# A squared-ReLU attention and Fourier-mix FFN kernel on one core: the first FFN layer of two token groups in two passes, with the hand-offs around it reordered

## The chip, the cores and the metric

The kernel runs on 1 core of one Trainium2 chip. The metric is the time of one execution in device microseconds (us); lower is better. The kernel before takes 610.42 us, the median of 3 runs (609.92 to 610.85).

## The reference

Eight batches of 448 tokens. Twelve heads of 64 attend with squared ReLU, the result is mixed by a two-dimensional Fourier transform of which the real part is kept, and a normalised FFN of width 3072 is added.

```python
scores = (1/sqrt(64)) * q @ k.T                  # per batch (8) and head (12), 448 x 448
x  = (maximum(scores, 0)**2 / 448) @ v           # heads side by side: x is 8 x 448 x 768
u  = x + real(fft(fft(x, axis=1), axis=2))
un = (u - mean(u)) / sqrt(var(u) + 1e-6)         # over the 768 features of a token
out = u + maximum(un @ w_ch1, 0) @ w_ch2         # 768 -> 3072 -> 768
```

## The kernel before

Data are bf16 for TensorE (PE) and f32 for `u` and the output. The names follow the data:

- `turn_on_pe` (batches 0 and 1) and `turning` (later ones) lay q and k out with the head dimension on partitions (`qkT`). On PE a set is 16 small matmuls into one `psF` bank, which VectorE (DVE) or ScalarE (ACT) copies out.
- `attention(b)` visits 24 score blocks of a batch, three at a time. A block is two matmuls at L537 into `psS`; ACT takes the ReLU (L558) and DVE squares it (L564) into one of nine `sq` buffers. A value set, eight matmuls at L522, uses four squares of an earlier visit; `lag` says how many visits old they must be. `fold` brings the result to SBUF (`xT`, L445 and L448).
- `mix(b)` multiplies by the channel table (L961), casts to `pc`, and `mix_rows(b, ch)` makes the rows of one half in two parts `ch`: matmuls at L805, `tm` and `tp` on DVE, `u` on DVE and GpSimd (POOL), statistics, `std`, `nmr`, and the normalised rows `un`. From batch 2 on `un` is stored to DRAM (`ntop`, `nbot`) and comes back turned by DMA as `unT`; for batch 1 PE turns it (`turn_rows`, L775).
- `first_tail` does all of this for batch 0 in an order written out by hand: four row tiles `t` (`rows`, L605 and L609), their statistics (L629), copies of `u` (L658), `un` (L682 on POOL, L684, L687), a turn on PE (L708) and an unload into `unT` (L723). At L706 and L713 it issues 24 matmuls on a constant tile, `warm`, between the turns.
- `ffn(b)` takes a group of 384 or 512 tokens, which alternate. FFN1 (L1073) is 24 output blocks `j` of six matmuls, each block a `psF` bank, then a ReLU to `hT` (L1044, L1046). FFN2 (L1091) is 48 matmuls for each 128 tokens, in two halves of 384 columns, each added to a reloaded `u` (`o`, L1054) and stored.

PSUM is held in three double banks (`BS`, tiles `psS`) and two single banks (`BF`, tiles `psF`). FFN1, FFN2, the value sets and the turned q and k all take turns on the two `psF` banks.

The order on each engine is fixed when the kernel is built. Every piece of work is a generator that asks for an engine, a duration, what it waits for and the buffers that it takes; `Streams.run` gives the engine to the piece that can begin first by its own cost functions, and keeps that order:

```python
def mm(n):
    return n / 2400 + 0.006
...
key = (ok is not None and not ok(), max(t), s[1][eng != "PE"])
```

`ok` in `attention` holds a visit back until the FFN has progressed far enough (`lead`); for batch 1 also until the tail of batch 0 is through (`tail`). On the chip each engine then works through its list in order, and a wait at its head holds all that is behind it. The DMA queues of SyncE (SP) and POOL are such lists too: a DMA on POOL waits until the one eight places before it has landed, and a second indirect store into the same DRAM tile waits for the first.

Of the kernel before, what the change touches and what calls it, by code (L numbers as in the profile page):

```python
# [12 lines left out]
ALU = mybir.AluOpType  # L13
# [104 lines left out]
def mm(n):  # L118
    return n / 2400 + 0.006
# [18 lines left out]
def kernel(  # L138
# [54 lines left out]
    back = [const.tile([128, 1], mybir.dt.int32, name=f"back{i}") for i in range(2)]  # L193
    warm = const.tile([128, 512], BF16, name="warm")
# [27 lines left out]
    def mirrors():  # L222
        nc.gpsimd.memset(rev, 0.0)
        nc.gpsimd.affine_select(out=rev, in_=rev, compare_op=ALU.not_equal, fill=1.0,
                                base=-127, pattern=[[1, 128]], channel_multiplier=1)
        nc.gpsimd.iota(back[0], pattern=[[0, 1]], base=HS, channel_multiplier=-1)

        v = const.tile([128, 2], FP32, name="backv")
# [253 lines left out]
    def attention(b):  # L482
# [5 lines left out]
        while pa < NB:  # L488
# [4 lines left out]
            lag = 3 if few else 1  # L493
# [18 lines left out]
            e = yield need("PE", dur + SWITCH, deps, bufs, lambda: progress[0] >= lead and (b != 1 or tail[0] == 2 or tail[0] == 0 and p < 0))  # L512
# [68 lines left out]
    def first_tail(pcs):  # L581


        pus, helds, done, sts = [None] * 4, [None] * 4, [[None, None] for _ in range(4)], [None] * 4
        mvs, stds, rss, nms, uts, pts = ([None] * 4 for _ in range(6))
        t_st, t_mv, t_std, t_rn = ([0.0] * 4 for _ in range(4))
        t_un, t_u = [[0.0, 0.0] for _ in range(4)], [[0.0, 0.0] for _ in range(4)]

        def rows(t):
            ch, i = divmod(t, 2)  # L590
            s0, s1 = SC[ch]
            n = s1 - s0
            d = 4 * mm(D // 2) + 3 * 0.06
            e = yield need("PE", 2 * d, [pcs[0][1], pcs[1][1]] + x_ready[0], [BF, BF] if t == 3 else [BS])
            if t == 3:
                pu = helds[t] = [BF.take() for _ in range(2)]
            else:
                helds[t] = [BS.take()]
                pu = [helds[t][0][:, 0], helds[t][0][:, 1]]
            for hf in range(2):  # L600

                for w in range(2):
                    for a, (n0, n1) in enumerate(TC):
                        mat = seq[:n1 - n0, w, a, s0:s1] if w == 0 or i ^ hf else nseq[:n1 - n0, a, s0:s1]
                        nc.tensor.matmul(pu[hf][:n, 0:D // 2], lhsT=mat,  # L605
                                         rhs=pcs[a][0][:n1 - n0, w, hf:hf + D // 2],
                                         start=(w == 0 and a == 0), stop=False)
                for a in range(3):
                    nc.tensor.matmul(pu[hf][:n, a * 128:(a + 1) * 128],  # L609
                                     lhsT=xTc[5 - a if hf else a][:, i * XH + s0:i * XH + s1],  # L610
                                     rhs=rev if hf else ident, start=False, stop=(a == 2))
                done[t][hf] = e - (1 - hf) * d + LATENCY["PE"]
            pus[t] = [p[:n] for p in pu]
            if t == 3:
# [5 lines left out]
        def half(t, hf):  # L620

            return pus[t][hf][:, D // 2 - 1::-1] if hf else pus[t][hf][:, 0:D // 2]

        def stats(t, hf):
            n = SC[t // 2][1] - SC[t // 2][0]
            t_st[t] = yield need("DVE", dve(D // 2), [done[t][hf]])
            if hf == 0:
                sts[t] = work.tile([128, 2, 6], FP32, name="stats", tag="stats", bufs=2)
            nc.vector.bn_stats(sts[t][:n, hf, :], pus[t][hf][:, 0:D // 2])  # L629

        def aggregate(t):
            n = SC[t // 2][1] - SC[t // 2][0]
            t_mv[t] = yield need("DVE", 0.2)
            mvs[t] = work.tile([128, 2, 2], FP32, name="mv", tag="mv", bufs=4)[:n]
            nc.vector.bn_aggr(mvs[t][:, 0, :], sts[t][:n])

        def root(t):
            n = SC[t // 2][1] - SC[t // 2][0]
            t_std[t] = yield need("ACT", 0.25, [t_mv[t] + LATENCY["DVE"]])
            stds[t] = work.tile([128, 2], FP32, name="std", tag="std", bufs=4)[:n]  # L640
            nc.scalar.activation(stds[t][:, 0:1], mvs[t][:, 0, 1:2], AF.Sqrt, bias=eps_t[:n])

        def scale(t):
            n = SC[t // 2][1] - SC[t // 2][0]
            e = yield need("DVE", 0.3, [t_std[t] + LATENCY["ACT"]])
            t_rn[t] = e + LATENCY["DVE"]
            rss[t] = work.tile([128, 2], FP32, name="rstd", tag="rstd", bufs=4)[:n, 0:1]
            nms[t] = work.tile([128, 2], FP32, name="nmr", tag="nmr", bufs=4)[:n, 0:1]
# [3 lines left out]
        def copy(t, hf, en):  # L652
            ch, i = divmod(t, 2)
            n = SC[ch][1] - SC[ch][0]
            e = yield need(en, (act if en == "ACT" else dve)(D // 2), [done[t][hf]], [BU[i]] if hf == 0 else [])
            if hf == 0:
                uts[t] = work.tile([128, D], FP32, name="u", tag=f"u{i}" if i else "u", bufs=2)
            (nc.scalar.copy if en == "ACT" else nc.vector.tensor_copy)(  # L658
                uts[t][:n, hf * (D // 2):(hf + 1) * (D // 2)], half(t, hf))
            t_u[t][hf] = e  # L660
            if t == 3:
                BF.give(helds[t][hf], e)
            if hf == 1:
                if t != 3:
                    BS.give(helds[t][0], max(t_u[t]))
                e = max(t_u[t])
                first_us[ch][i] = uts[t], e + LATENCY["ACT"], e
                u_done[ch][i].t = e + LATENCY["ACT"]

        def norm(t, hf, en):  # L670
            ch, i = divmod(t, 2)
            n = SC[ch][1] - SC[ch][0]
            deps = [t_rn[t]]
            if en == "POOL":
                deps.append(u_done[ch][i])
            d = {"ACT": act(D // 2), "DVE": dve(D // 2), "POOL": 2.0}[en]
            e = yield need(en, d, deps, [BUN[ch]] if i == 0 and hf == 0 else [])
            if uns[0][t] is None:
                uns[0][t] = work.tile([128, D], BF16, name="un", tag=f"un{t}", bufs=1)
            un = uns[0][t][:n]  # L680
            if en == "POOL":
                nc.gpsimd.tensor_scalar(un, uts[t][:n], rss[t], nms[t], op0=ALU.mult, op1=ALU.add)  # L682
            elif en == "ACT":
                nc.scalar.activation(un[:, hf * (D // 2):(hf + 1) * (D // 2)], half(t, hf), AF.Identity,  # L684
                                     bias=nms[t], scale=rss[t])
            else:
                nc.vector.tensor_scalar(un[:, hf * (D // 2):(hf + 1) * (D // 2)], half(t, hf), rss[t], nms[t],  # L687
                                        op0=ALU.mult, op1=ALU.add)
            t_un[t][hf] = e + LATENCY[en]
            if min(t_un[t]) or en == "POOL":  # L690
                half_un[ch][i].t = max(t_un[t])

        def turned_cols(t):

            return ((128, ident, 0, 128), (128, rev[:, 0:63], HS + 97, 63),
                    (96, ident[:96, :96], 128, 96), (97, rev[:97, 31:128], HS, 97))[t]

        def turn(t, k):
            n, idn, c0, w = turned_cols(t)
            un = uns[0][t]  # L700
            e = yield need("PE", 6 * 0.06 + 0.11 * k, [max(t_un[t])], [BS])
            pts[t] = [BS.take()]
            bank = [pts[t][0][:, 0], pts[t][0][:, 1]]
            for i in range(k):

                nc.tensor.matmul(bank[0][:, 0:256], lhsT=warm[:, 0:128], rhs=warm[:, 0:256], start=True, stop=True)  # L706
            for m in range(MC):
                nc.tensor.matmul(bank[m // 3][:, m % 3 * 128:m % 3 * 128 + w], lhsT=un[:n, m * 128:(m + 1) * 128],  # L708
                                 rhs=idn, start=True, stop=True)
            done[t] = [e + LATENCY["PE"]] * 2  # L710
            for i in range(16 if t == 1 else 0):

                nc.tensor.matmul(bank[0][:, 384:512], lhsT=warm[:, 0:128], rhs=warm[:, 0:128], start=True, stop=True)  # L713
            if t == 1:
                yield need("PE", 16 * 0.055)

        def unload(t, en):
            n, idn, c0, w = turned_cols(t)
            g = groups[0][2]
            src = pts[t][0][:, :, 0:384].rearrange("p h (m w) -> p h m w", w=128)[:, :, :, 0:w]  # L720
            dst = g[:, :, c0:c0 + w].rearrange("p (h m) w -> p h m w", h=2)
            last = yield need(en, (act if en == "ACT" else dve)(6 * w), [done[t][0]])
# [440 lines left out]
```

## Time and profile before

| what | value |
|---|---|
| median of 3 runs | 610.42 us (609.92 to 610.85) |
| span of the profiled execution, first to last instruction | 607.4 us |
| PE busy | 595.4 us, 98% of the span |
| DVE, ACT, POOL busy | 339.4, 293.3, 155.2 us |
| FFN1, FFN2 on PE (L1073, L1091) | 227.2, 225.0 us |
| scores, value sets on PE (L537, L522) | 52.3, 45.9 us |
| first FFN1 matmul of group 0, of group 1, of group 2 | 53.74, 126.67, 210.84 us |
| PE idle after the first FFN1 matmul, up to 604.0 us | 4.73 us |

The profile gives the execution by its span alone; the runs' median stands 3.0 us above it, and that is taken as what lies around the span. A profile line has the start (us), the duration (us), the engine, the source line, the operation, what it writes and reads, how many, and in brackets how long the engine had been idle before it and what ended that wait. A matmul's duration includes the time in which the next ones already run; the distance from one start to the next is what it costs PE.

### The profile page before, as it was taken

The page shows a single profiled execution, that of the slowest core. Times are in us where ns is not written, and L with a number is a line of the kernel's source. Part 1 is how long each engine was busy: PE and PEld are TensorE (multiplying, and loading weights), DVE is VectorE, ACT ScalarE, POOL GpSimd, SP SyncE. Part 2 cuts the span into 40 slices and gives each one's busy share as a digit, 9 for nine tenths or more (in the row PEclk, how much of TensorE's full clock was granted, in tenths as well). Part 3 has the DMA queues.
Part 4 walks back from the last instruction along what each step waited for, and adds up shares of the span by engine and source line. Part 5 has one row for each costly group of instructions (what it writes and reads, how often), then busy time and mean ns, then how long its engine had stood idle before and what let it go on. Part 6 is the DMA issues. An engine that isn't in the chain of part 4 may idle for free.

```text
span 607.4 us, 10224 instructions
## 1 busy us (share of the span) xinstructions
PE 595.4 (98%) x4035; PEld 329.5 (54%) x4054; DVE 339.4 (56%) x766; ACT 293.3 (48%) x445; POOL 155.2 (26%) x200
## 2 busy tenths in 40 slices
PE   8999999989999999999999999999999999999997
PEld 7566556534555565555445565555445566654464
DVE  6977785876596568455834369645843447110011
ACT  5967661677544357436653167435761345014300
POOL 8433203311163137111710117210620006100000
PEclk9999999999999999999999999999999999999999
DMA  9999997888659967977593796985451215420022
GB/s 127 207 209 228 216 194 132 186 128 120 111 148 212 157 121 215 141 135 120 172 154 96 127 127 173 160 164 97 145 136 60 87 51 165 121 91 20 1 79 79
DMA packets 125216, 82.22 MB, mean 135 GB/s; under 512 B 76272, under 2 KB 113168, under 8 KB 125168
## 3 DMA queue, kind: packets, MB, share of 16 engines
q0 software_dynamic: 40320, 34.07, 34.4%
q1 hardware_dynamic: 84848, 47.50, 33.6%
q8 instruction: 32, 0.52, 0.4%
q14 instruction: 16, 0.13, 0.1%
HBM read 62.91 MB, written 26.69 MB: 148 GB/s over the span
## 4 chain that ended last, share of the span: by engine, by line
PE 83%; DVE 11%; ACT 4%; issue 1%; DVEq 0%; ACTq 0%
PE psF L1091 33%; PE psF L1073 32%; PE psF L522 6%; PE psS L537 6%; DVE sq L564 2%; PE psS L961 2%; ACT sq L558 2%; DVE stats L837 2%; PE psS L1113 1%; PE psS L805 1%; DVE u L826 1%; DVE u L825 1%; PE psS L605 1%; PE psF L421 1%; DVE tm L816 1%
## 5 line engine op out<-in xcount | busy, mean ns | idle before, releaser
L1073 PE MATMUL psF<-unT,w 128*128 128x384 bf16 (+1 forms) x1134 | 227.2, 352 | 1.4 <-issue 0.2
L558 ACT ACTIVATE sq<-psS 112x896 bf16<-112x896 f32 x192 | 164.8, 916 | 130.5 <-PE psS L537 130.4
L1091 PE MATMUL psF<-w,hT 128*128 128x384 bf16 (+2 forms) x1343 | 225.0, 326 | 0.8 <-DVE xT L448 0.7
L1091 PEld LDWEIGHTS <-hT 128*128 128x128 bf16 x1344 | 129.2, 98 | 93.4 <-issue 8.8
L1073 PEld LDWEIGHTS <-w 128*128 128x128 bf16 x1152 | 109.6, 98 | 109.3 <-issue 12.3
L1046 ACT ACTIVATE hT<-psF 128x512 bf16<-128x512 f32 (+1 forms) x180 | 98.6, 548 | 110.2 <-PE psF L1073 109.6
L564 DVE TENSOR_TENSOR sq<-sq 112x896 bf16<-112x896 bf16 x192 | 117.8, 635 | 44.6 <-ACT sq L558 43.3
L1054 DVE TENSOR_TENSOR o<-psF,o 128x384 f32<-128x384 f32 (+2 forms) x56 | 31.0, 553 | 106.2 <-PE psF L1091 105.9
L300 POOL DMA_DIRECT2D vn<-in_v_dram x24 | 17.3, 719 | 177.4 <-PE psF L522 156.9
L445 DVE TENSOR_SCALAR xT<-psF 128x224 bf16<-128x224 f32 x48 | 18.7, 389 | 71.7 <-PE psF L522 71.7
L537 PE MATMUL psS<-qkT 64*112 64x448 bf16 x384 | 52.3, 366 | 2.0 <-DVE unT L780 0.8
L522 PE MATMUL psF<-sq,vn 112*64 112x448 bf16 x384 | 45.9, 359 | 1.7 <-DVE sq L564 1.2
L825 POOL TENSOR_TENSOR u<-tp,xn 128x385 f32<-128x385 f32 (+1 forms) x14 | 15.5, 1108 | 117.0 <-DVE tp L816 94.7
L537 PEld LDWEIGHTS <-qkT 64*112 64x112 bf16 x384 | 20.8, 125 | 27.6 <-issue 21.6
L522 PEld LDWEIGHTS <-vn 112*64 112x64 bf16 x384 | 17.9, 109 | 24.2 <-issue 16.0
L854 POOL TENSOR_SCALAR un<-u,rstd,nmr 128x768 bf16<-128x768 f32 (+1 forms) x24 | 26.9, 1124 | 6.4 <-DVE nmr L846 6.0
L837 DVE BATCH_NORM_STATS2 stats<-u 128x6 f32<-128x384 f32 (+1 forms) x56 | 28.2, 539 | 0.0
L879 POOL DMA_INDIRECT ubot<-u,back x16 | 17.1, 1072 | 23.7 <-DVE hT L1044 19.3
L300 POOL DMA_DIRECT2D qn<-in_q_dram x21 | 15.3, 726 | 19.7 <-DVE qkr L389 10.8
L1113 PE MATMUL psS<-warm 128*128 128x126 bf16 (+1 forms) x204 | 17.9, 242 | 1.3 <-DVE warm L215 1.3
L448 DVE TENSOR_SCALAR xT<-psF 128x224 bf16<-128x224 f32 x48 | 18.4, 384 | 0.0
L456 DVE TENSOR_TENSOR fold<-xT 128x225 bf16<-128x225 bf16 x48 | 15.9, 331 | 2.1
(117 smaller groups left out, 369.1 us busy)
## 6 DMA issues: line engine op xcount, KB each, us to landing
out_dram<-o SPq DMA_DIRECT2D x27, 384.0 KB, 2.7
vn<-in_v_dram POOLq DMA_DIRECT2D x24, 224.0 KB, 5.0
qn<-in_q_dram POOLq DMA_DIRECT2D x21, 224.0 KB, 6.3
kn<-in_k_dram POOLq DMA_DIRECT2D x21, 224.0 KB, 7.2
w<-in_moe_w_ch_dram POOLq DMA_DIRECT2D x12, 384.0 KB, 14.1
w<-in_moe_w_ch_dram POOLq DMA_DIRECT2D x4, 1152.0 KB, 22.7
utop<-u SPq DMA_DIRECT2D x8, 384.0 KB, 2.6
o<-utop SPq DMA_DIRECT2D x8, 384.0 KB, 4.5
```

The costliest lines, as they stand in the source:

```text
L300: nc.gpsimd.dma_start(out=t, in_=src[b, hs].rearrange("h (p j) d -> p h (j d)", j=4))
L522: nc.tensor.matmul(av[h * Dh:(h + 1) * Dh, 0:S], lhsT=vn[:, c, h0 + h, :], rhs=sq[:, h, :], start=(c == 0), stop=(c == 3))
L537: nc.tensor.matmul(sc[:R, h, 0:S].rearrange("k (c q) -> k c q", c=4), lhsT=kT[ps, m % 2, c, :], rhs=qT[ps, m % 2], start=True, stop=True)
L558: nc.scalar.activation(r, sc[:R, :, 0:S], AF.Relu)
L564: nc.vector.tensor_tensor(r, r, r, op=ALU.mult)
L837: nc.vector.bn_stats(stats[:n, hf, :], u[:n, hf * (D // 2):(hf + 1) * (D // 2)])
L854: nc.gpsimd.tensor_scalar(un[:n], u[:n], rstd[:n, i:i + 1], nmr[:n, i:i + 1], op0=ALU.mult, op1=ALU.add)
L1046: nc.scalar.activation(h[:, 0:N], ph[:, 0:N], AF.Relu)
L1054: nc.vector.tensor_tensor(o[:, hs], pc[:, 0:w], o[:, hs], op=ALU.add)
L1073: nc.tensor.matmul(ph[:, 0:N], lhsT=w1_sb[m][hf][:, jj * 128:(jj + 1) * 128], rhs=unT[:, m, 0:N], start=(m == 0), stop=(m == MC - 1))
L1091: nc.tensor.matmul(pc[:, 0:w], lhsT=hT[j][:, c * 128:(c + 1) * 128], rhs=w2_sb[j // 6][:, j % 6, hs], start=(j == 0), stop=(j == JC - 1))
L1113: nc.tensor.matmul(first_pps[0][:, t, c0:512], lhsT=warm[:, 0:128], rhs=warm[:, c0:512], start=not begun, stop=False)
```

## The change

**Cost function.** `mm` adds 0.002 instead of 0.006, which moves the planned order in all batches.

**Batch 0's tail.** Each half row is a step of its own. Tile 0 lies in the two `psF` banks, tile 1 in two double banks, one a half; tiles 2 and 3 lie each in one double bank with both halves. Tile widths become 128, 128, 96, 96 (before: 128, 128, 112, 112). `un` of tiles 0 and 1 is made half on ACT, half on DVE, no longer on POOL. The turn goes into the bank that the row came from. Tiles 2 and 3 are streams of their own behind the first FFN1 matmuls: two copies on ACT, then two statistics, and POOL makes `un`. The constant matmuls of L706 and L713 are gone. The row stores wait for the copies; both indirect stores also wait for tile 3's `un`.

**FFN1.** Group 0 is done in a pass over 128 tokens (four blocks `j` in a bank), which needs tile 0 alone, and a pass over 256 (two blocks). Group 1 is done in two passes of 256, the first of which needs three of its five parts. `hT` becomes six tiles of four blocks. The tokens of both groups are in another order, so reloads and stores of `o` are cut into `pieces`.

**Attention.** `lag` is 2 for batches 1 and 2; batch 1 no longer has early work before the tail; batch 2 waits until batch 1's last rows are placed.

```diff
-    return n / 2400 + 0.006
+    return n / 2400 + 0.002
...
-            lag = 3 if few else 1
+            lag = 3 if few else 2 if b < 3 else 1
...
-            e = yield need("PE", dur + SWITCH, deps, bufs, lambda: progress[0] >= lead and (b != 1 or tail[0] == 2 or tail[0] == 0 and p < 0))
+            e = yield need("PE", dur + SWITCH, deps, bufs, lambda: progress[0] >= lead and (b != 1 or tail[0] == 2) and (b != 2 or un_ready[1][1].t is not None))
...
+        widths = (128, 128, R - 16, R - 16)
...
+        def rows(t, hf):
+            i, n = t % 2, widths[t]
+            pool = BF if t == 0 else BS
...
+            pu = held[t][-1][:n] if t == 0 else held[t][-1][:n, hf if t > 1 else 0]
...
+        def store(t):
+            ch, i = divmod(t, 2)
+            n = widths[t]
+            if i:
+                e = yield need("POOL", 1.1, [copied[t], used[3]])
+                nc.gpsimd.indirect_dma_start(
...
-        for t in range(3):
-            yield from rows(t)
-            if t == 2:
-                yield from rows(3)
-            yield from stats(t, 0)
-            if t:
-                yield from scale(t - 1)
-                yield from norm(t - 1, 0, "POOL")
-            yield from stats(t, 1)
-            yield from aggregate(t)
-            yield from copy(t, 0, "ACT")
-            yield from root(t)
-            yield from copy(t, 1, "ACT")
...
-        yield from turn(1, 5)
-        yield from norm(3, 0, "ACT")
-        yield from unload(1, "DVE")
-        yield from turn(2, 3)
...
+        def later(t):
+            for hf in range(2):
+                yield from stats(t, hf)
+            yield from aggregate(t)
+            yield from root(t)
+            yield from scale(t)
+            yield from norm(t, None)
+            for hf in range(2):
+                yield from turn(t, hf)
+            for hf in range(2):
+                e = yield from unload(t, hf)
...
+        yield from run(((rows, 0, 0), (stats, 0, 0), (rows, 0, 1), (copy, 0, 0), (stats, 0, 1), (aggregate, 0),
+                        (copy, 0, 1), (root, 0), (rows, 1, 0), (stats, 1, 0), (scale, 0), (norm, 0, 0), (norm, 0, 1),
+                        (rows, 1, 1), (stats, 1, 1), (aggregate, 1), (rows, 2, 0), (turn, 0, 0), (turn, 0, 1),
+                        (copy, 1, 0), (root, 1), (copy, 1, 1), (scale, 1), (unload, 0, 0), (unload, 0, 1), (rows, 2, 1),
+                        (norm, 1, 0), (norm, 1, 1), (turn, 1, 0), (turn, 1, 1), (unload, 1, 0), (unload, 1, 1)))
         tail[0] = 2
-        sch.add(turn_rows(uns[0][1], max(t_un[1]), 128, rev[:, 63:127], 0, 64, "DVE", second_un[0]), (1, 1))
+        for t in (2, 3):
+            if t == 3:
+                for hf in range(2):
+                    yield from rows(t, hf)
+            sch.add(copies(t), (0.05 * t, 0.05 * t))
+            sch.add(later(t), (0.05 * t, 0.05 * t))
...
+            yield need("SP", 0.0, second_un[:3])
+            group_ready[1].t = max(c.t for c in second_un[:3])
...
-            for t0, n in ((0, 384), (384, 512)):
+            for segs, n in (([(0, 128), (HS + 96, 128), (128, 128)], 384), ([(256, 64), (S, 128), (S + 384, 64), (S + 320, 64), (S + 128, 192)], 512)):
...
-        for j in range(JC):
-            hf, jj = divmod(j, JC // 2)
-            e = yield need("PE", 6 * mm(N), [w1_ready[hf]], [BF])
-            ph = BF.take()
-            for m in range(MC):
-                nc.tensor.matmul(ph[:, 0:N], lhsT=w1_sb[m][hf][:, jj * 128:(jj + 1) * 128],
-                                 rhs=unT[:, m, 0:N], start=(m == 0), stop=(m == MC - 1))
...
+        def first(k, c0, w, ready=()):
+
+            for j0 in range(0, JC, k):
+                hf = j0 // (JC // 2)
+                for i in range(k):
...
+                    for m in range(MC):
+                        nc.tensor.matmul(ph[:, i * w:(i + 1) * w], lhsT=w1_sb[m][hf][:, jj * 128:(jj + 1) * 128],
+                                         rhs=unT[:, m, c0:c0 + w], start=(m == 0), stop=(m == MC - 1))
...
+        if b == 0:
+            yield from first(4, 0, 128, first_un[:1])
+            e = yield from first(2, 128, 256, first_un)
+        elif b == 1:
+            yield from first(2, 0, 256)
+            e = yield from first(2, 256, 256, second_un)
+        else:
+            e = yield from first(1, 0, N)
```

More of the change, by code (lines that the diff above doesn't have):

```diff
@@ L670, in norm @@
[L670 to L706, printed above, removed]
-            for m in range(MC):
[L708 to L722, printed above, removed]
-            (nc.scalar.copy if en == "ACT" else nc.vector.tensor_copy)(dst, src)
-            BS.give(pts[t][0], last)
-            first_un[t].t = last + LATENCY["ACT"]
+            cp(uts[t][:widths[t], hf * (D // 2):(hf + 1) * (D // 2)], half(t, hf))
@@ new lines, in turn, with unload @@
+        def turn(t, hf):
+            n = widths[t]
+            e = yield need("PE", 3 * 0.06, [t_un[t][hf]])
+            for m in range(3 * hf, 3 * hf + 3):
+                nc.tensor.matmul(banks[t][hf][:, m % 3 * 128:m % 3 * 128 + n], lhsT=uns[t][:, m * 128:(m + 1) * 128],
+                                 rhs=rev[:n, 128 - n:] if t % 2 else ident[:n, :n], start=True, stop=True)
+            t_turn[t][hf] = e + LATENCY["PE"]
+        def unload(t, hf):
+            n = widths[t]
+            en, cp = (("ACT", nc.scalar.copy), ("DVE", nc.vector.tensor_copy))[hf]
+            e = yield need(en, (act, dve)[hf](3 * n), [t_turn[t][hf]])
+            src = banks[t][hf][:, 0:384].rearrange("p (m w) -> p m w", w=128)
+            for g, c0, w0, w1 in ((0, t * 128, 0, n),) if t < 3 else ((0, 352, 0, 32), (1, 0, 32, 96)):
+                cp(groups[g][2][:, 3 * hf:3 * hf + 3, c0:c0 + w1 - w0], src[:, :, w0:w1])
+            if t < 2:
+                (BF, BS)[t].give(held[t][hf], e)
+            unloaded[t].append(e + LATENCY[en])
+            if len(unloaded[t]) == 2:
+                first_un[t].t = max(unloaded[t])
+                if t > 1:
+                    BS.give(held[t][0], max(unloaded[t]))
+            return e
@@ L727, in first_tail, with run @@
+        def run(steps):
+            for step, t, *hf in steps:
+                yield from step(t, *hf)
         tail[0] = 1
```

266 lines of the change are left out of this document (141 added, 125 removed).

## The prediction

> **What bounds the kernel now.** I read the page first, then the stretches, then PE's waits and timeline, last the other engines around the places where PE waits.
>
> ```profile
> PE 595.4 (98%) x4035; PEld 329.5 (54%) x4054; DVE 339.4 (56%) x766; ACT 293.3 (48%) x445; POOL 155.2 (26%) x200
> PEclk9999999999999999999999999999999999999999
> ```
>
> PE is the bound, so an edit pays only by taking work off PE or by filling a place where PE waits or runs constants.
>
> ```profile
> 48.00:53.70 5.70, 4.44 (x77) 3.67 (x75) 4.59 (x14) 4.65 (x10) 3.49 (x4) 1.00 1.13 260
> 53.70:90.00 36.30, 35.79 (x284) 19.14 (x279) 27.71 (x62) 25.86 (x37) 5.27 (x7) 1.00 1.22 213
> 90.00:126.70 36.70, 34.52 (x249) 20.55 (x249) 28.30 (x63) 15.49 (x21) 10.33 (x12) 1.00 0.75 153
> 126.70:200.00 73.30, 72.38 (x439) 35.62 (x442) 48.31 (x109) 43.01 (x63) 21.42 (x25) 1.00 0.83 146
> ```
>
> Length less PE's busy time: 1.26 us idle in batch 0's tail, 0.51 in group 0, 2.18 ahead of group 1, 0.92 up to 200 us; from 200 to 604 only 1.12 more. The constants of L706 and L713 in the tail take 0.55, 0.89 and 0.33 us. All that this change could win is therefore 3.0 us in the tail and some 3.6 us behind it.
>
> **The two places.** PE's timeline (start, duration, what; in brackets the idle time before it):
>
> ```profile
> 49.05 1.06 PE L713 MATMUL psS<-warm 128*128 128x128 bf16 x16
> 51.60 0.44 PE L708 MATMUL psS<-rev,un 97*128 97x97 bf16 x6 [0.91 <-ACT un L684]
> 57.45 4.07 PE L1073 MATMUL psF<-unT,w 128*128 128x384 bf16 x24
> 122.58 0.40 PE L537 MATMUL psS<-qkT 64*112 64x448 bf16 x2 [0.83 <-DVE unT L780]
> 124.89 0.38 PE L522 MATMUL psF<-sq,vn 112*64 112x448 bf16 x2 [1.04 <-DVE sq L564]
> 179.70 3.10 PE L1091 MATMUL psF<-w,hT 128*128 128x384 bf16 x18 [0.70 <-DVE xT L448]
> ```
>
> At 122 to 125 us FFN2 of group 0 is used up, group 1 is not complete, and what is left of attention waits for DVE.
>
> **PE's work: about the same.** Starts of successive groups give the price of a matmul. 128 columns: 16 at L713 in 0.89 us, 55.6 ns. 256 columns: 5 at L706 in 0.55 us and 24 at the end of L1091 in 2.6 us, 108.7 ns. 384: 96 at L1073 in 15.7 us, 162.5 ns less its changes. 512: 144 in 31.0 us, 215.3 ns. A change of the kind of work adds 0.10 us (6 of 384 take 1.08).
> I compare what is left in before at its first FFN1 matmul, 53.74 us, with what is left in the changed order of instructions at the turn of tile 2. There group 0's FFN1 has 120 of 128 and 144 of 256 columns left: 6.67 + 15.65 = 22.32 us against 144 x 162.5 ns = 23.40, that is -1.08. Group 1: 288 x 108.7 = 31.30 against 31.00, +0.30. Two turns of 96 rows +0.54, one score block more +0.19, one q-and-k set less -0.52, four more changes of work +0.40. Sum -0.17; I take -0.1. Before leaves 604.1 - 53.74 - 4.73 = 545.6 us of work there, so after leaves 545.5.
>
> **The tail: 0.8 us lost.** Up to 41.06 us nothing differs. The eight half rows go at 0.83 us each. Tile 0, which now has banks of its own, has statistics to 43.79, `nmr` at 44.96, `un` in halves on ACT and DVE (0.68 each, L684 and L687) to 45.68, its turn at 45.73, its unload at 47.10 on ACT and 47.58 on DVE. FFN1 begins at 47.15, six microseconds earlier, with PE waits of 0.22, 0.26 and 0.31. After three blocks come tile 3's rows (48.90 to 50.55), a q-and-k set, a score block and FFN1's fourth block, to 51.73. The next q-and-k set needs a `psF` bank; one is held by FFN1's first four blocks, the other by the first set, until DVE copies it out (L426, 0.61). On DVE that copy stands behind all statistics of tiles 2 and 3, and these are slow for this reason:
>
> ```profile
> 43.23 1.03 DVE L629 BATCH_NORM_STATS2 stats<-psS 128x6 f32<-128x384 f32 x2 [1.41 <-PE psS L609]
> 44.37 0.48 ACT L658 COPY u<-psS 128x384 f32<-128x384 f32 x1 [1.30 <-DVE stats L629]
> 54.22 0.61 DVE L426 COPY qkT<-psF 128x896 bf16<-128x896 bf16 x1
> ```
>
> The first half of that double bank was written by 42.36, yet both readers waited for the whole tile and for one another. Tile 3 sits in such a bank: from 50.75, copy 0.48, statistics 0.57, copy 0.48, statistics 0.57, with 0.05 at each hand-off, to 53.0; then `rstd`, `nmr` and an aggregate for 0.33 and the copy, 53.95. PE waits 2.25 us with everything queued behind it; the set takes 0.52, and the turn of tile 2 comes at 54.55 (POOL's `un`, 0.98 from 53.38, is just in time). That is 0.81 us later than 53.74. If the halves went separately, tile 3 would be 0.5 us earlier: 54.05, the other end.
> The Trainium skill, page "PSUM — Partial Sum Buffer", section "PSUM bank collisions raise a hardware error", asks for a guard between two engines only on the same bank (and quarter of the partitions). By it the halves, which are two banks, need not wait for each other, and the sum would be 0.5 us less. The trace's 43.23 speaks against that here.
>
> **Group 0, 54.5 to 88 us: nothing.** A bank of FFN1 now fills in 1.33 us (24 x 55.6 or 12 x 108.7) and its ReLU of 512 columns takes 0.60 on ACT (L1046) and, from 0.56 for 384, some 0.69 on DVE; they alternate. Copies of `u`, statistics and unloads of tiles 2 and 3 lie under it. I find no wait; the old 0.51 is the other end.
>
> **The step to group 1: 2.2 us won, 0.4 paid.** Adding up pieces puts MIX at 99.0, `mix_rows` at 103.15 and the end of FFN2 at 118.27. In before the last row statistics of batch 1 ended 16.3 us after `mix_rows` began (99.61 to 115.95); without the 1.60 us of squares and a copy between them it is 117.6. ACT's two unloads for the first three parts then end at 118.65: a wait of 0.4 (0 to 1.5). The late `un` (ACT, to 120.8) is needed only by the second pass. Held scores and older squares leave PE with FFN1 to do where it waited for DVE.
>
> **Downstream.** 126.7 to 200: the 0.70 at L1091 came from a value set amid batch 2's rows; that set now comes 13 us instead of 11 after them. I keep 0.3 of 0.92. Group 2 starts at 205.6 instead of 210.84, and its rows begin 10 us later than before, so its DMA chain gets tight:
>
> ```profile
> 190.03 1.21 SPq L477 DMA_TRANSPOSE xn<-xT  x1
> 193.40 1.26 SPq L902 DMA_TRANSPOSE unT<-ntop  x1
> 196.79 1.23 SPq L902 DMA_TRANSPOSE unT<-nbot  x1
> unT<-nbot SPq DMA_TRANSPOSE x9, 4.3
> ```
>
> On SP these two stand right behind the third `xn` transpose of batch 3, at 199.4 to 199.9: 1.2 each, the second issued at 201.8 to 202.4, landing 4.3 later, 206.1 to 206.7. PE waits 0.5 to 1.1 (0 to 1.4 with the drift of both); I take 0.7. From then on the order repeats the old cycle: 1.1.
>
> **Hidden edits.** The last `w1` load lands at 44.4 (29.77 + 14.6), before FFN1. The fourth `w2` load moves ahead of POOL's `un` and both indirect stores behind it: the second lands near 84.5 (78.9 before). SP's reload of `o` waits for it with the third `xn` transpose behind it, which is ready at 82 and wanted by 105; past that, each us of it would delay batch 1's `u`. Two more iotas (0.13 each) lie at 15 us. More, smaller DMAs for `o` go through a queue that is free; `hT` in six tiles frees at the same matmuls.
>
> **The sum.** Start 54.55 + work 545.5 + waits (0 + 0.4 + 0.3 + 0.7 + 1.1 = 2.5) + what follows the last matmul, 3.3 = 605.9 us of span; before, by the same terms, 53.74 + 545.6 + 4.73 + 3.3 = 607.4. That is 1.5 us less, and with the 3.0 between span and median, 608.9 us, -0.25%. About 0.2%, 1.2 us, is what a measurement here can tell from no change: faster is below 609.2, slower above 611.6. With its small terms the forecast goes from 607.9 to 609.9: chance 0.50, 0.36 of it faster.
>
> **Rivals.**
> *More won* (0.12): tile 3's halves go separately and group 2 lands in time: -0.5 - 0.7, 607.7, with 0.5 more from group 1's start and the stretch to 200 down to 606.8.
> *The wait only moves* (0.16; 0.10 the same, 0.06 slower): group 1's last unload or group 2's transposes come 1.5 us later than I walked and the time is 610.4; against it, no sum above has so much missing; for it, ACT and DVE are within 0.5 us of PE at both.
> *The clock, slower* (0.12): the constants that kept PE busy in the tail are gone, and PE now waits 2.25 us at once. The page's clock row never falls, but matmuls of 126 columns at L1113 take 310 ns until 6.4 us and 218 ns at 12 us, with starts 107 and 59 ns apart: after idleness PE is half as fast for 5.4 us. Should the wait bring that back, it costs 2.7 us and the time is 611.6, where it begins to count as slower. Against it: after the waits of 0.91 and 1.04 us nothing is slow.
> The Trainium skill, page "TensorE: Matmul & The Clock Gate", Part 1, has the clock halved after a window of about 3.4 us without work. By that a wait of 2.25 us would not do it; no run here shows where the limit lies.
> *Weights bind narrow matmuls* (0.04): a load lasts 98 ns (PEld at L1073); if each of 144 matmuls of 128 columns took that, +6.1 us, 615. Against it: L708 issued six of 63 columns, each with a load, in 0.17 us.
> *Group 2's chain breaks* (0.06): `nbot` stands behind a v load on POOL; a landing 3.4 us later than walked gives 611.6 or more.
>
> **How the numbers follow.** Faster 0.36 + 0.12 = 0.48, same 0.14 + 0.10 = 0.24, slower 0.06 + 0.12 + 0.04 + 0.06 = 0.28. The range goes from the better rival's end, 606.8, to the clock's case with 0.7 more, 612.3.
>
> **What would show it.** Right: first FFN1 matmul near 47.2; PE idle over 2 us ahead of a q-and-k set at 54, ended by DVE's copy; group 1's FFN1 at 118 to 119; group 2's at 206 with a wait of under 1.1. Wrong: 128-column starts further apart than 56 ns, PE waits over 1 us at 118, or `unT` landing past 208.

## The result, and the profile after

The changed kernel takes 617.25 us, the median of 6 runs (614.05 to 621.14); the kernel before takes 610.22 us in the same measurement (609.10 to 610.87, 6 runs). The ratio is 1.0123 (95% interval 1.0102 to 1.0145): slower by 1.2%, where 608.9 us (606.8 to 612.3) was forecast. Before's runs lie within 1.8 us of each other, after's spread over 7.1 us. The profiled execution of after has a span of 614.0 us and a time of 615.79 us.

The page of after, lines of parts 1, 2 and 5 (in the last: group of instructions, count, busy time, mean ns, idle time before it and what ended most of it):

```profile
PE 595.6 (97%) x4314; PEld 348.9 (57%) x4314; DVE 337.8 (55%) x766; ACT 295.2 (48%) x448; POOL 154.3 (25%) x201
PEclk9999999999999899999999999999999999999999
L1085 PE MATMUL psF<-unT,w 128*128 128x256 bf16 (+3 forms) x1440 | 231.4, 317 | 8.8 <-DMA unT<-nbot 7.3
```

PE has as much to do as before (595.4), as forecast. The clock row, all nines before, has an 8 in the fourteenth slice, and FFN1 now waits 7.3 us for a DMA, at one place.

The same stretches as before the change, and the two behind them (length, then busy time and count of PE, PEld, DVE, ACT and POOL, the granted clock, DMA share, GB/s):

```profile
48.00:53.70 5.70, 3.90 (x56) 3.15 (x54) 3.85 (x12) 3.60 (x9) 0.38 (x1) 1.00 1.15 256
53.70:90.00 36.30, 36.21 (x414) 27.11 (x413) 25.54 (x56) 25.02 (x37) 8.04 (x10) 1.00 1.09 194
90.00:126.70 36.70, 36.36 (x279) 24.00 (x278) 25.22 (x56) 14.76 (x24) 9.72 (x11) 1.00 0.95 163
126.70:200.00 73.30, 73.30 (x572) 47.71 (x572) 49.41 (x112) 41.45 (x59) 21.51 (x24) 1.00 0.80 134
200.00:216.00 16.00, 8.73 (x50) 4.33 (x49) 8.63 (x21) 6.98 (x9) 2.09 (x3) 0.79 1.26 171
216.00:300.00 84.00, 84.00 (x544) 45.61 (x543) 55.72 (x127) 46.85 (x74) 26.89 (x29) 1.00 0.81 150
```

Before, the last two stretches were:

```profile
200.00:216.00 16.00, 16.00 (x107) 8.82 (x104) 10.09 (x27) 6.60 (x10) 3.01 (x5) 1.00 0.90 159
216.00:300.00 84.00, 83.65 (x530) 45.32 (x531) 56.14 (x123) 46.95 (x76) 30.24 (x32) 1.00 0.74 149
```

From 53.7 to 200 us the change does what it was walked to do: between 90 and 126.7 us PE idles 0.34 us where it idled 2.18, and between 126.7 and 200 not at all, where it idled 0.92. In the tail PE idles 0.54 us more than before (1.80 against 1.26). Nearly all of the loss lies from 200 to 216 us: 7.27 us idle, where before had none, and a granted clock of 0.79.

PE's timeline at the three places where the prediction expected waits (start, duration, what; in brackets the idle time before):

```profile
53.79 0.39 PE L424 MATMUL psF<-ident,qn 112*64 112x112 bf16 x8 [1.89 <-DVE qkT L429]
117.90 0.50 PE L1085 MATMUL psF<-unT,w 128*128 128x256 bf16 x3 [0.34 <-DVE unT L780]
212.90 3.68 PE L1085 MATMUL psF<-unT,w 128*128 128x384 bf16 x12 [7.27 <-DMA unT<-nbot]
```

The first two came as forecast (2.25 and 0.4). The third is group 2's FFN1, forecast with 0.7. It also starts at half speed: its first 12 matmuls take 3.68 us.

What stands behind the third, on SP, DVE and POOL, in order of time:

```profile
197.04 0.93 SPq L866 DMA_DIRECT2D ntop<-un  x1
200.79 0.43 DVE L392 COPY qkr<-kn 112x1024 bf16<-112x1024 bf16 x1 [2.21 <-DMA qkT<-qkr]
201.13 0.38 DVE L448 TENSOR_SCALAR xT<-psF 128x224 bf16<-128x224 f32 x1
201.84 1.22 SPq L480 DMA_TRANSPOSE xn<-xT  x1
203.55 1.33 SPq L892 DMA_TRANSPOSE unT<-ntop  x1
204.97 1.26 SPq L892 DMA_TRANSPOSE unT<-nbot  x1
205.23 0.71 POOL L303 DMA_DIRECT2D vn<-in_v_dram  x1 [7.71 <-PE psF L525]
```

The value set whose result goes to `xT` ended on PE near 198.5. DVE reached it only at 201.13, because a copy of k stood ahead of it and waited 2.21 us until an earlier `qkT` transpose had let go of `qkr`. So the third `xn` transpose, walked at 199.4 to 199.9, is issued at 201.84, and both `unT` transposes stand behind it on SP. The first of them also needs the `ntop` store, and by the profile that landed only at 203.46, 6.4 us after its issue at 197.04 and 0.09 us before the transpose went. So without the copy of k the first transpose would still not have gone before 203.5. In e4 below the store landed at 202.08, and the transpose went at 203.22, right behind `xn`: each of the two links alone explains nearly all of the late issue. No run took the copy of k out of the way.
The second transpose is issued at 204.97, and PE goes on at 212.90, 7.9 us later, where 4.3 was walked. 0.26 us after its issue POOL begins to issue 672 KB of q, k and v for batch 4, released by the value set just ahead of FFN1.

### The profile page after: what moved, and what is told of

The parts are those of the page before. It is cut to its first block, busy times and chain, and to the rows that moved or that the text cites. A ratio compares the mean times of both kernels' runs of the same rounds, so it can differ in the third digit from the quotient of the medians.

```text
span 614.0 us, 10759 instructions
## 1 busy us (share of the span) xinstructions
PE 595.6 (97%) x4314; PEld 348.9 (57%) x4314; DVE 337.8 (55%) x766; ACT 295.2 (48%) x448; POOL 154.3 (25%) x201
## 4 chain that ended last, share of the span: by engine, by line
PE 79%; DMA 8%; DVE 6%; POOL 3%; issue 3%; ACT 1%; SPq 0%; POOLq 0%; DVEq 0%; ACTq 0%
PE psF L1085 34%; PE psF L1113 29%; PE psS L540 5%; PE psF L525 5%; DMA w<-in_moe_w_ch_dram 2%; PE psS L954 2%; DMA qn<-in_q_dram 2%; DVE stats L826 2%; DMA unT<-nbot 1%; DMA kn<-in_k_dram 1%; PE psS L794 1%; DMA vn<-in_v_dram 1%; DVE u L815 1%; POOL qk L303 1%; DMA out_dram<-o 1%
## 5 line engine op out<-in xcount | busy, mean ns | idle before, releaser
L1085 PE MATMUL psF<-unT,w 128*128 128x256 bf16 (+3 forms) x1440 | 231.4, 317 | 8.8 <-DMA unT<-nbot 7.3
L1085 PEld LDWEIGHTS <-w 128*128 128x128 bf16 x1440 | 132.4, 98 | 101.1 <-issue 23.3
L303 POOL DMA_DIRECT2D kn<-in_k_dram x21 | 15.2, 725 | 6.8 <-DVE qkr L392 3.2
L1135 PEld LDWEIGHTS <-warm 128*128 128x128 bf16 x206 | 12.8, 104 | 6.3 <-issue 4.6
```

The costliest lines, as they stand in the source:

```text
L303: nc.gpsimd.dma_start(out=t, in_=src[b, hs].rearrange("h (p j) d -> p h (j d)", j=4))
L1085: nc.tensor.matmul(ph[:, i * w:(i + 1) * w], lhsT=w1_sb[m][hf][:, jj * 128:(jj + 1) * 128], rhs=unT[:, m, c0:c0 + w], start=(m == 0), stop ...
L1135: nc.tensor.matmul(first_pps[0][:, t, c0:512], lhsT=warm[:, 0:128], rhs=warm[:, c0:512], start=not begun, stop=False)
```

## The experiments

All kernels below are the changed kernel with the edit shown, except the last, which is the kernel before with one. Each was compared with the kernel before on the same chip; before had medians of 609.3 to 609.4 us there. Line numbers shift by a few with an edit. Three theories were at stake. A: the chain from batch 2's MIX (the channel product, L954) to group 2's `unT` is longer than the distance that PE's order leaves. B (later D): the transposes land late because of the loads issued beside them. C: an idle PE loses its clock, and this has a price beyond the wait.

**e1: the planner's constant alone taken back.**

```diff
-    return n / 2400 + 0.002
+    return n / 2400 + 0.006
```

> The changed kernel with one constant of the planner as before: a matmul of n columns counts n/2400 + 0.006 instead of + 0.002. The order that comes out has MIX of batch 2 about 4 us earlier on PE (166.7 against 170.7 by piece prices) and group 2's FFN1 at the same place (206.8). Theory A (the DMA chain from batch 2's rows to group 2's unT is too long for the place that FFN1 has: 43.4 us from MIX at 169.5 to the landing at 212.9, where PE gives it 36.1): the wait of 7.3 falls to about 3.3, the clock row no longer falls (1.5 us), span 614.0 - 4.0 - 1.5 = 608.5. Theory B (the chain would be in time, the two transposes land late, 7.9 us instead of 4.4, because the q, k and v loads of batch 4 are issued in the same 2 us): the wait stays at 6 to 7 us, span 613 to 614.

Measured: 610.81 us (608.36 to 616.78, 12 runs), ratio 1.0020 (0.9997 to 1.0042). In the profiled run (span 609.7) the wait for `unT` is 2.05 us; the transpose is issued at 202.91, 1.20 us ahead of the v load, and lands after 5.7. That is A's side, but the runs spread over 8 us, which a distance alone doesn't do. And the clock fell at another place. Windows of e1:

```profile
51.00:54.00 3.00, 1.11 (x24) 0.88 (x22) 2.42 (x7) 2.01 (x5) 0.98 (x1) 1.00 1.13 255
54.00:57.40 3.40, 3.40 (x36) 3.38 (x35) 1.24 (x5) 1.21 (x2) 2.85 (x3) 0.50 1.26 205
57.40:60.00 2.60, 2.60 (x42) 2.12 (x41) 1.10 (x3) 1.36 (x4) 0.00 (x0) 0.99 1.17 212
```

After the tail's wait of 1.89 us (in e1 it ends at 53.46) PE runs 3.4 us at half clock: 1.7 us of work lost.

**e2: constant and `lag` taken back.** As e1, and

```diff
-            lag = 3 if few else 2 if b < 3 else 1
+            lag = 3 if few else 1
```

> The changed kernel with the planner's constant back at 0.006 and value sets on squares one visit old (lag 1) in batches 1 and 2, as before; the hold and the two passes stay. MIX of batch 2 comes at 164.8 and group 2's FFN1 at 208.4, 43.6 us apart by piece prices against 36.1. Theory A: that is as long as the chain took (43.4), wait 0 to 1, no fall of the clock, span 614.0 - 7.0 - 1.5 = 605.5 (605.2 to 606.5). Theory B: the loads of batch 4 still come with the value set just before FFN1, wait 5 or more, span 611 to 614.

Measured: 611.71 us (608.65 to 617.59, 12 runs), ratio 1.0040 (1.0012 to 1.0068). The profiled run (608.4) has no wait for `unT`: the transpose, issued at 203.31 and 0.89 us ahead of the v load, lands after 5.0. The tail has its half clock from 53.3 to 56.7. Other runs have spans from 606.9 to 615.8, where A expected 605.2 to 606.5; what the longer ones waited for was not traced. One order on PE gives all of these times, so A in its simple form, one fixed length of the chain, falls here.

**e3: constants in front of group 2's FFN1.**

```diff
+                    for _ in range(28 if b == 2 and j == 0 else 0):
+                        nc.tensor.matmul(ph, lhsT=warm[:, 0:128], rhs=warm, start=True, stop=True)
```

> The changed kernel with 28 matmuls of 512 constant columns (28 x 0.2153 = 6.0 us) put on PE right ahead of group 2's first FFN1 matmul; nothing else moves. It tells what the wait costs beyond its own length. If PE's clock falls because PE has had nothing to do for 3.6 us: the wait left is 7.3 - 6.0 = 1.3 us, the clock row stays at 1.00 from 205 to 220, FFN1's first 12 matmuls of 384 columns take 2.0 us instead of 3.68, span 614.0 - 1.5 = 612.5. If the slow stretch is not from idleness (power, DMA traffic): the clock row still falls near 209 and span stays 614.0.

Measured: 616.60 us (616.04 to 616.69, 4 runs), ratio 1.0105 (1.0085 to 1.0126). PE's timeline and two of its windows:

```profile
206.71 6.22 PE L1082 MATMUL psF<-warm 128*128 128x512 bf16 x27
215.03 2.12 PE L1087 MATMUL psF<-unT,w 128*128 128x384 bf16 x12 [2.10 <-DMA unT<-nbot]
209.00:212.00 3.00, 3.00 (x16) 1.37 (x14) 1.53 (x3) 0.00 (x0) 0.00 (x0) 1.00 1.25 88
212.00:215.00 3.00, 0.92 (x5) 0.20 (x2) 0.00 (x0) 0.00 (x0) 0.00 (x0) 1.00 1.55 171
```

With PE kept busy the clock stays at 1.00 and the same 12 matmuls take 2.12 us instead of 3.68: in after, idleness cost 1.56 us at this place beside the wait itself. The span did not fall to 612.5, because the transposes landed later (8.8 us after issue, 0.15 us ahead of the v load) and the tail lost its clock in this run.

**e4: batch 4's loads held back until group 2's first ReLU.**

```diff
+        if i == 4 * NG + 1:
+            yield need("POOL", 0.1, [late])
+            nc.gpsimd.tensor_copy(scrap, late_h[0])
```

(`late` and `late_h` are set by that ReLU to its end and to two columns of `hT`.)

> The changed kernel with the second q, k and v loads of batch 4 (issued at 205.2 to 206.6, while group 2's unT transposes of 203.55 and 204.97 are on their way) held on POOL until the first ReLU of group 2 is done, by a copy of two columns of hT there. Up to group 2 PE's order is the same. Theory A with no part for crowding: the transposes land as late as before, wait 7.3, span 614.0. Theory B: unT<-nbot lands 4.4 us after its issue instead of 7.9, wait 3.8, the clock hardly falls (0 to 0.2), span 614.0 - 3.5 - 1.5 = 609.0.

Measured: 621.53 us (618.01 to 622.73, 6 runs), ratio 1.0180 (1.0155 to 1.0206). The wait on POOL stands ahead of five loads: the three that after issues from 205.23 on, and a q and a k load that it issues at 196.02. As a version it is worse: with these 7 and 15 us late the planner's order changes from 226 us on, and PE waits 2.1 and 4.1 us at 244 and 280, each with its stretch of half clock. But at group 2 it answers what it was made for. The transpose is issued at 204.64, with no load near it:

```profile
208.64 2.11 PE L1093 MATMUL psF<-unT,w 128*128 128x384 bf16 x12 [1.89 <-DMA unT<-nbot]
```

It lands 4.0 us after its issue, against 7.9. The wait is 5.4 us shorter than after's, more than the 3.5 expected: 3.9 by the landing, and 1.4 because the transpose is issued 34.0 us after MIX (170.61) instead of 35.5.

**e8 and e9: the hold taken back too.** e8 has the constant of e1 and no hold, e9 also the `lag` of e2.

```diff
-... and (b != 1 or tail[0] == 2) and (b != 2 or un_ready[1][1].t is not None))
+... and (b != 1 or tail[0] == 2))
```

> The changed kernel with the planner's matmul constant at 0.006 and without the hold of batch 2's scores; value sets stay two visits old. MIX of batch 2 comes at 164.8 and group 2's FFN1 at 208.3 by piece prices, 43.5 us apart (before 52.1, after 36.0, e1 40.0). Theory A (distance from MIX to FFN1 against a DMA chain that takes about 43): group 2's wait is 0 to 1 us. Group 1's FFN1 is 1.3 us later in PE's order (120.5) since scores of batch 2 stand ahead of it again, and some of the 1.87 us that before waited for DVE at 122 to 125 comes back. With the half clock of 3.4 us in the tail (1.7 us, in three runs of four so far) the span is 607 to 608.5, without it 605.5 to 606.8. Rival (what e2 showed was not the distance but chance: its runs went from 606.9 to 615.8 at a distance of 43.6): runs spread over more than 5 us again.

> The changed kernel with all three changes of the planner's attention taken back (constant 0.006, no hold, lag 1): what is left is the new tail and FFN1 of groups 0 and 1 in two passes. MIX of batch 2 at 160.3 and group 2's FFN1 at 208.3, 48.0 us apart. Theory A: no wait for unT at group 2 in any run, so the runs agree within 3 us (only the tail's half clock of 3.4 us, 1.7 us, comes and goes), span 605.2 + 0.5 to 1.5 for waits on DVE at group 1 + 0 or 1.7: 606 to 608.5. Rival (the loss sits in the new tail or the two passes themselves): span stays above 610.

Measured: e8 610.19 us (607.78 to 611.98, 12 runs), ratio 1.0006 (0.9990 to 1.0021); e9 610.85 us (609.69 to 612.26, 10 runs), ratio 1.0019 (1.0007 to 1.0031). In e8's profiled run `unT` lands 8.1 us after its issue at 204.43, 0.68 us ahead of the v load, and PE waits 2.4 us, where A expected 0 to 1, although MIX came 4.3 us earlier than in after (165.22 against 169.50). e8's spans still spread over 4.2 us (606.0 to 610.2). In e9 nothing waits for `unT`, and its runs agree within 2.6 us, at spans of 607.9 to 610.5, a little above what was expected. What e9 has left, the new tail, the two passes and batch 1 without early work, does not by itself beat before: with the three edits gone, waits on DVE come back (0.57 at 119, 0.68 at 165, 0.49 at 178, 0.80 at 214).

**g1 and g9: the tail's wait filled.** e1 and e9 with the last FFN1 block ahead of that wait issued four more times over the same columns:

```diff
+                    for m in list(range(MC)) * (4 if b == 0 and c0 == 0 and j == 3 else 0):
+                        nc.tensor.matmul(ph[:, i * w:(i + 1) * w], lhsT=w1_sb[m][hf][:, jj * 128:(jj + 1) * 128],
+                                         rhs=unT[:, m, c0:c0 + w], start=(m == 0), stop=(m == MC - 1))
```

> e1 with the last six FFN1 matmuls ahead of the tail's wait for a psF bank (128 columns, the fourth block of group 0's first bank) issued four more times over the same columns: 24 x 55.6 ns = 1.33 us of the wait of 1.89 us filled with repeated work, nothing else moved. Theory C (a stretch of 3.4 us in which PE stands idle for about half already halves the clock for the next 3.4 us, 1.7 us lost; e1 to e4 all show it at 53 to 57 us): the wait at 53.5 is 0.5, the clock row stays at 1.00 in the tail, runs with a mean clock of 0.997 become rare, and the median falls by 1.3 us (three quarters of 1.7) against e1's 610.8, to 609.5. Rival (the half clock has another cause, such as the matmuls of 128 columns themselves): the clock still falls near 54 and the median stays at 610.8.

> e9 with the same 24 repeated matmuls in the tail. If both causes are right (the distance from batch 2's rows to group 2, and the tail's half clock), neither wait nor half clock is left: mean clock 0.999 to 1.000 in nearly all runs, span 605.7 to 606.7, against 607.4 before: ratio 0.997 to 0.999. If only the distance was right, it equals e9.

Measured: g1 608.43 us (606.56 to 613.15, 12 runs), ratio 0.9998 (0.9976 to 1.0020); g9 608.93 us (608.54 to 609.92, 11 runs), ratio 0.9990 (0.9981 to 0.9999). PE in g1:

```profile
51.32 1.50 PE L1088 MATMUL psF<-unT,w 128*128 128x128 bf16 x24
53.38 0.39 PE L424 MATMUL psF<-ident,qn 112*64 112x112 bf16 x8 [0.55 <-DVE qkT L429]
```

Of g1's 12 runs 8 have a mean clock of 0.999 or 1.000, of e1's 3; all 11 of g9's have. The median falls by 2.4 us (e1 to g1; 1.3 expected) and 1.9 (e9 to g9). C holds in the tail too. g9's spans, 606.8 to 608.1, are about 1 us above those expected (e9's were 2 us above); g1's still go from 604.8 to 611.4.

**h1 and h2: the loads behind the landing.** h1 is g1, and h2 the changed kernel with the repeated matmuls, both with

```diff
+        if i == 4 * NG + 1:
+            yield need("POOL", 0.1, [group_ready[2]])
+            nc.gpsimd.tensor_copy(scrap, groups[2][2][:, 0, 300:302])
```

> g1 (the changed kernel, planner's constant 0.006, 24 repeated matmuls in the tail) with one wait more on POOL: the second q, k and v loads of batch 4 are issued only when group 2's unT has landed, by a copy of two columns of unT there. PE's order is g1's. Theory D: what varies from run to run is how long the last unT transpose takes to land, and that hangs on how soon after it the loads are issued (lead of the transpose over the v load and its landing so far: e3 0.15 us and 8.8 us, after 0.26 and 7.9, e8 0.68 and 8.1, e1 1.20 and 5.7, before 3.08 and 4.3, e4 no load and 4.0). Then it lands 4.0 to 4.4 us after its issue here, group 2's wait is under 1 us in every run, all runs lie between 605 and 607 us of span with a mean clock of 0.999 to 1.000, ratio to before 0.995 to 0.997. Rival (the landing varies with the traffic that is there anyway, xn and qkT transposes and o): the runs go up to 611 as g1's do.

> The changed kernel itself (constant 0.002) with the two edits of h1: repeated matmuls in the tail, loads of batch 4 behind unT's landing. It tells the two parts of group 2's wait of 7.3 us apart. Theory D: the landing falls from 7.9 to 4.2, the issue stays 35.5 us after MIX of batch 2, so the wait is 3.6 (2.8 to 4.0) in place of 7.3, and the clock may still halve for one stretch of 3.4 us, 1.7 us: span 614.0 - 3.7 - 0 to 1.5 = 608.8 to 610.3, still slower than before's 607.4. If the loads were the whole cause: span 605.5 to 606.5. If they play no part: 612.5 to 614.

Measured: h1 607.44 us (607.01 to 607.98, 9 runs), ratio 0.9970 (0.9960 to 0.9980): faster than before, and all runs within 1 us, where g1's had 6.6. The transpose lands after 5.3 us, though, where 4.0 to 4.4 was expected, at 205.64, 0.14 us before FFN1 begins. PE's waits from 200 to 300 us in h1, none of them ended by `unT`:

```profile
PE psF L1089 <- DVE o L1060: 0.9, 1, 0.9
PE psF L1089 <- ACT hT L1051: 0.4, 1, 0.4
```

h2: 611.46 us (611.24 to 612.12, 5 runs), ratio 1.0037 (1.0024 to 1.0051); span 609.7, inside the 608.8 to 610.3 expected.

```profile
208.25 3.55 PE L1089 MATMUL psF<-unT,w 128*128 128x384 bf16 x12 [2.88 <-DMA unT<-nbot]
```

PE goes on 4.1 us after the issue of the transpose at 204.12. Against after the wait is 4.4 us shorter: 3.8 by the landing, and 0.6 because the transpose is issued 34.9 us after MIX (169.24) instead of 35.5, in a run in which the two loads of 196 us were held as well. The other 2.9 us are the late issue, which stays, and they still cost a stretch of half clock: with the loads held and the tail's wait filled, the change in full is still slower than before.

**h3: one part alone, on the kernel before.**

```diff
-... (b != 1 or tail[0] == 2 or tail[0] == 0 and p < 0))
+... (b != 1 or tail[0] == 2 or tail[0] == 0 and p < 0) and (b != 2 or un_ready[1][1].t is not None))
```

> The kernel before with one part of the change alone: batch 2's scores held until batch 1's rows are normalized. Group 1's FFN1 stands 3 us earlier in PE's order, MIX of batch 2 9.5 us later, group 2's FFN1 at the same place: 42.5 us from MIX to FFN1 by piece prices against 52.1. By what the runs of the changed kernel showed (issue of the last transpose 35.5 to 39 us after MIX, landing 4 to 8 more: 40 to 47) the wait at group 2 is 0 to 4 us and runs differ; the waits of 0.83 and 1.04 us on DVE at 122 to 125 are gone or halved. Span 606 to 611, median 0 to 2 us above before's. Rival (the hold is harmless to group 2 and pays by itself): span 605.5 to 606.5 in all runs.

Measured: 607.12 us (606.56 to 607.97, 5 runs), ratio 0.9966 (0.9952 to 0.9979). The rival was right, and the wait of up to 4 us at group 2 did not come: the hold pays by itself. Windows of h3:

```profile
90.00:126.70 36.70, 36.24 (x252) 21.41 (x252) 25.64 (x57) 14.99 (x21) 9.73 (x11) 1.00 0.86 153
200.00:216.00 16.00, 15.56 (x105) 8.02 (x102) 12.35 (x31) 8.76 (x13) 3.65 (x6) 1.00 1.40 180
```

Between 90 and 126.7 us PE idles 0.46 us where before had 2.18: 1.7 of the 1.9 us by which the profiled spans differ (605.5 against 607.4). MIX of batch 2 moves from 157.92 to 164.85 and the last transpose from 196.79 to 201.79, but here it is 1.68 us ahead of the v load, FFN1 stands at 208.42, and nothing waits for `unT`.

## Why the prediction was wrong

**The sum against the trace.** By the same terms, after is: start 54.35 + work 545.8 + waits 8.5 + half clock 1.6 + what follows the last matmul 3.8 = 614.0 (the work is what is left up to the last matmul's end at 610.2). The prediction had 54.55 + 545.5 + 2.5 + 0 + 3.3 = 605.9. Start, work and the end are off by -0.2, +0.3 and +0.5. The waits of group 0 (0), of the step to group 1 (0.34), up to 200 us (0) and behind group 2 (0.86) add up to 1.2 where 1.8 was allowed. The whole miss is group 2's wait for `unT`, in the sum at 0.7 us (0 to 1.4): it is 7.27 us, and 1.56 more for the clock behind it, which the sum did not have.

**The step that failed** is the walk of group 2's chain. It said itself that the chain "gets tight", and was wrong in two of its rows. The second transpose, walked as issued at 201.8 to 202.4, was issued at 204.97. The third `xn` transpose ahead of it, "at 199.4 to 199.9", came at 201.84, since DVE was not free for that value set: the walk went along SP's list and PE's, not through DVE's list, where a copy waits for a DMA to release its buffer. And the `ntop` store, which the walk does not mention, landed at 203.46. The other row is "landing 4.3 later": 7.9. The 4.3 was the page's median over the nine `nbot` transposes, and was carried to a moment at which PE's new order puts the loads of batch 4 beside it. h2 splits the wait of 7.27 us: 3.8 go away with the loads behind the transpose, 0.6 with an earlier issue, and 2.9 stay. What made the issue late is read from the trace alone.
Before's own trace held the warning. Its `nbot` transposes landed after 2.5 to 8.9 us, and the two slowest, at 216.8 (6.5) and 387.1 (8.9), are the two with q, k and v loads issued in the 3.6 us ahead of them; its first two `ntop` stores landed after 2.9 and 6.1 us. The upper end of 1.4 took in only the drift of the start.

**The tail** came as walked: first FFN1 at 47.02 (47.15), wait 1.89 (2.25), turn of tile 2 at 54.35 (54.55). That DVE's statistics and ACT's copies of a double bank follow each other held too: the trace has "[0.53 <-ACT u L663]" ahead of tile 3's statistics at 51.22.

**The step to group 1** was right in size, 1.8 us won between 90 and 126.7. Of its reasons the held scores are enough: h3 has 1.7 us of it without new tail or passes. h1, which has the change with the constant taken back, the tail's wait filled and the loads held, is no faster (0.9970, 0.9960 to 0.9980, against 0.9966, 0.9952 to 0.9979). What the new tail loses and what the passes win was not measured apart.

**The rival "Group 2's chain breaks" (0.06)** is what happened, by another link: the v load on POOL did not hold up `nbot`, whose store was issued right behind it and landed 5.9 us later, in time. The later loads slowed the transpose.

**The rival "The clock, slower" (0.12)** is real as well. It was priced at 5.4 us at half clock after the 2.25 us wait. Measured: 3.4 us, 1.7 us of work, in the profiled runs of e1 to e4 and e8. In after's own profiled run the tail kept its clock and group 2 lost it.

**The rival "Weights bind narrow matmuls" (0.04)** did not come: 36 matmuls of 128 columns fill the 2.01 us from 54.62 to 56.63 in after, 56 ns each.

**Span and median.** The 3.0 us between them was read as lying around the span. In the results every run's time is 1.8 above its own span. The rest was spread among runs: later measurements of before put 13 of 33 runs at a mean clock of 0.993 to 0.997 and spans of 608.3 to 610.4, the others at 607.1 to 607.9. What PE waits for in those runs was not traced.

## What to carry to other kernels

When an edit moves work towards a hand-off by DMA, walk that chain through every queue that it crosses, buffers released by other DMAs included, and ask which loads are on their way when its last transfer is issued, or are issued within the next microsecond. Read the spread of a landing time and not its median alone. Here a wait of some 2 us on PE cost up to 1.7 us more than its length, and repeated matmuls in it won that back. Try each part of a large change alone: here one condition on one line gives as much as the best of the larger versions (h3 against h1).

## What the runs showed of the hardware

**A transpose that is followed at once by loads lands twice as late.** The last `unT` transpose of group 2: lead over the v load on POOL, and time from issue to landing (where PE waited for it, to the end of that wait).

| kernel | lead, us | landing, us |
|---|---|---|
| e3 | 0.15 | 8.8 |
| after | 0.26 | 7.9 |
| e8 | 0.68 | 8.1 |
| e2 | 0.89 | 5.0 |
| e1 | 1.20 | 5.7 |
| before | 3.08 | 4.3 |
| e4 | load after landing | 4.0 |
| h2 | load after landing | 4.1 |
| h1 | load after landing | 5.3 |

Between a lead of 0.68 and one of 0.89 us the landing changes by 3 us, which fits the spread of e1, e2 and g1 and its end in h1.
The traces of all kernels here together give 67 `nbot` transposes with a landing time; their pieces differ in size. 18 of them had a q, k or v load issued between 2.5 us ahead of them and 0.2 us behind: they landed after 6.2 to 10.1 us. 43 had no such load near, or only loads that were issued at least 0.9 us behind them or had landed at most 0.3 us behind: 2.5 to 5.6 us, with e1, e2 and h1 among them (e1 by its landing time, 5.6). The other six had loads issued longer before, some still on their way: 3.9 to 8.8 us. The Trainium skill, page "DMA: Bandwidth & Descriptors", section "Queues, rings and completion order", lets each DMA engine take turns between the queues that have work for it, packet by packet. By that, a transfer that is joined by another queue's at its beginning would take up to twice as long, and one that is nearly through would not; the two ranges, 6.2 to 10.1 us and 2.5 to 5.6, agree. Why a load 0.9 us behind no longer counts, when the transpose is far from through, stays open.

**Half clock comes in stretches of 3.4 us, for less idleness than thought.** It lasted 3.4 us in the tails of e1 to e4 and e8, at h2's group 2 (207.8 to 211.2) and in e4 at 244.6, and 6.8 us in after (209.28 to 216.11) and in e4 at 278.7. In the 3.4 us ahead of each fall PE had been idle 1.81 us (e2), 1.89 (e1, e3, e4, e8), 2.28 and 3.00 (e4's later two), 2.42 (h2) or all the time (after). In after's tail the same wait of 1.89 us left the clock at 1.00, and so it was, by their mean clock, in 3 of e1's 12 runs: whether such a wait costs 1.7 us differs from run to run.
The Trainium skill, page "TensorE: Matmul & The Clock Gate", Part 1, has a free-running window of 3413 ns and half clock after an idle one. The lengths agree with the window; that it must be idle throughout does not: 53% (1.81 of 3.41) was enough. Counted back from after's fall at 209.28 in 46 windows of the page's length, an estimate, a window's edge lies at 52.27 and cuts the tail's wait (51.90 to 53.79) into 0.37 and 1.52 us; by that 45% was not enough, and the phase would explain why runs differ. The share of idle time alone does not decide, though: at the end of after PE is idle for 1.86 us (54%) of the window from 608.64 to 612.05, and the clock fell only one window later, at 615.47.
